# A reordered load phase: layer norms, filler projections and the first V rows in front of a 64-segment recurrence

## The chip, the core and the metric

The kernel runs on one core of a Trainium2 chip. The metric is device time in microseconds (us) of one execution. TensorE is PE below (its weight loads PEld), VectorE is DVE, ScalarE is ACT, GpSimd is POOL, and SyncE is SP, which only issues transfers. Each engine works through its own instructions in the order in which they were recorded. "SPq" or "POOLq" in a profile is the engine's sequencer issuing a transfer.

## What is computed

Two blocks follow one another on x (2048 rows of 512). Block A is attention over 64 segments of 32 rows, with a memory of 8 rows that each segment passes to the next:

```
x1 = layernorm(x)
mem = mem0
for s in 0..63:
    h = concat(mem, x1[32 s : 32 s + 32])            # 40 rows
    q, k, v = h Wq, h Wk, h Wv                       # 32 heads of 128
    p = softmax(mask(q k^T * 128**-0.5))             # 40 x 40 per head
    o = (p v) Wo                                     # 40 x 512
    mem = o[:8];  out_A[32 s : 32 s + 32] = o[8:]
h = x + out_A
```

Block B is a gated feed-forward block with a mixing matrix over the rows: z = gelu(layernorm(h) w_in), the second half of z is normalized, mixed over all 2048 rows by w_sp, increased by b_sp and multiplied with the first half; the result times w_out is added to h. The change does not touch block B.

## The kernel before

**Segments.** A segment's 40 rows are handled as 32 (8 memory rows and the first 24 rows of x) and 8 extended rows (the last 8 of x). The extended rows don't depend on the memory, so their projections are made ahead, for 16 segments at once, a "chunk" of 128 rows (chunks 0 to 3). `hTe` holds a chunk's transposed rows, `QTx` the projected Q and K. A group of `qkx_mm` (L390, matmuls L398) makes 4 heads of Q (i = 0 to 7) or of K (i = 8 to 15) with 16 matmuls; `vx_mm` (L411, matmuls L417) makes 512 columns of V (n = 0 to 7), also with 16. V of the extended rows goes through DRAM to change its layout: `vx_evac` (L421) copies PSUM to SBUF and stores to `vext_d` (L434), and `load_vx` (L439, issue L441) brings one segment's block to `Vx`. Segment s needs 8 consecutive rows of the chunk, that is partitions 8 i to 8 i + 7 of every store, with i = s mod 16.

**Load phase.** SP issues the first x block (L305), Wq in four quarters, the second x block (L308), three further x blocks, the first memory, Wk, Wv and Wo in four quarters each. A quarter is 1 MB and serves 8 heads, that is two groups of `qkx_mm`, or two of `vx_mm`. `ln_inplace` (L349) normalizes one x block: on DVE bn_stats (L352) and bn_aggr (L353), on POOL the reciprocal root (L354, L356), on DVE again the subtraction and multiplication (L358). Statistics alternate between two buffers. `xT` (L361) transposes a block on PE, and ACT copies it out (`xe_copy`, L379, for chunk rows, `ring_copy`, L374, for segment rows).

`start_group` (L710) makes a group into one of the PSUM banks 2, 3, 4, 5 in turn and evacuates it with ACT or DVE in turn; a V group that ACT evacuates is stored through ACT's queue, one that DVE evacuates through POOL's. The loop at L727 runs chunk 0's 16 groups; after group 5 and group 7 it normalizes blocks 1, 4, 5 and 6, and it adds groups 0 to 3 of chunk 1 from group 9 on:

```python
        if i == 5:
            ln_inplace(1)
            ln_inplace(4)
        if i == 7:
            ln_inplace(5)
            ln_inplace(6)
            late_consts()
...
        if i >= 9 and i % 2 == 1:
            start_x(1, i // 2 - 4)
```

**Segment loop.** L821 is written out by hand for all 64 segments. PE does QK (L464, 64 matmuls), the scores (L494 to L509), V (L558), the row sums (L524, L529), the product PV (L575 with the segment's own rows, L581 with `Vx`), the output projection `Wo` (L608), and `mem_out` (L627), whose result ACT writes as the next segment's memory (L630). Segment 0 also makes chunk 0's eight V groups (L842 to L865), issues the first two `load_vx` on POOL (L880), and makes groups 4 to 7 of chunk 1 (L882) ahead of PV. `part_evac` (L619) writes segment s's output to `part[s % 8]`; the same buffers hold chunk 0's V groups on their way to DRAM.

Two lists fill gaps on PE. `gx` (L777, L795 to L799) holds whole groups, one per segment, made ahead of PV into PSUM bank 3 (`XB`) and evacuated by DVE; `gv` (L800) holds V groups of chunks 2 and 3 cut into quarters of 4 matmuls, poured in around `mem_out`. In front of PV in segment 0 stands the first entry of `gx`, V group 0 of chunk 1.

The recording layer (`Emitter`, L34) derives all waits from named reads and writes; an engine waits in front of the instruction that needs them, and everything behind it on that engine waits too. A store through SP stands in SP's order with all other transfers that SP issues.

Of the kernel before, what the change touches and what calls it, by code (L numbers as in the profile page):

```python
# [169 lines left out]
def fast_path(nc, st, keep, A_x, A_mem0, A_Wq, A_Wk, A_Wv, A_Wo, A_seg_len, B_w_in, B_w_sp, B_b_sp, B_w_out, out):  # L170
# [27 lines left out]
    def sb(name, shape, dt):  # L198
        return st.enter_context(nc.sbuf_tensor("f_" + name, shape, dt))
# [42 lines left out]
    stats = sb("stats", [128, 2, 6], F32)  # L242
    mv = sb("mv", [128, RB, 2], F32)
    rstd = sb("rstd", [128, RB], F32)
    st1 = sb("st1", [128, 2, 6], F32)
    mv1 = sb("mv1", [128, 2, 2], F32)
    rs1 = sb("rs1", [128, 2], F32)
    mhalf = sb("mhalf", [128, RB], F32)
    okt = sb("okt", [128, RB], F32)
    okb = sb("okb", [128, 1], BF)  # L250
# [25 lines left out]
    def dve(fn, **k):  # L276
        return em.add("dve", fn, **k)
# [16 lines left out]
    def load_xe(ck, j):  # L294
        t, tok = xbuf(j)
        sp(lambda e: e.dma_start(t, xe[CK * ck:CK * ck + CK, XM:SEG, :]), writes=tok)
# [6 lines left out]
        em.mark_const(("W", mi, hq))  # L303

    load_xe(0, 0)  # L305
    for hq in range(4):
        load_w(0, hq)
    load_xe(1, 1)  # L308
    load_x(0, 4)
    load_x(1, 5)  # L310
    load_xe(2, 6)
# [34 lines left out]
                                                  fill=NEG, base=0, channel_multiplier=-1), reads=["mask"], writes=["mask"])  # L346


    def ln_inplace(j):  # L349
        t, tok = xbuf(j)  # L350
        k = j % 2
        dve(lambda e: e.bn_stats(out=st1[:, k, :], in_=t), reads=tok, writes=[("st1", k)])  # L352
        dve(lambda e: e.bn_aggr(out=mv1[:, k, :], in_=st1[:, k, :]), reads=[("st1", k)], writes=[("mv1", k)])  # L353
        pool(lambda e: e.tensor_scalar(out=rs1[:, k:k + 1], in0=mv1[:, k, 1:2], scalar1=EPS, scalar2=None, op0=ALU.add),  # L354
             reads=[("mv1", k)], writes=[("rs1", k)])
        pool(lambda e: e.tensor_tensor(out=rs1[:, k:k + 1], in0=rs1[:, k:k + 1], in1=mhalf[:, 0:1], op=ALU.pow),  # L356
             reads=[("rs1", k), "mhalf"], writes=[("rs1", k)])
        dve(lambda e: e.tensor_scalar(out=t, in0=t, scalar1=mv1[:, k, 0:1], scalar2=rs1[:, k:k + 1], op0=ALU.subtract, op1=ALU.mult),  # L358
            reads=tok + [("mv1", k), ("rs1", k)], writes=tok)

    def xT(j, bank):  # L361
        t, tok = xbuf(j)
# [58 lines left out]
    def vx_evac(ck, n, bank, eng="act", queue="sp"):  # L421
        if ck == 0:
            t, tok = part[:, n, :], [("part", n, 0), ("part", n, 1)]
        else:
            j = vcnt[0] % 2
            vcnt[0] += 1
            t, tok = Vs[:, j, :], [("Vs", j)]
        if eng == "act":
            act(lambda e: e.activation(out=t, in_=ps[:, bank, :], func=ACT.Copy), reads=[PB(bank)], writes=tok)
        else:  # L430
            dve(lambda e: e.tensor_copy(out=t, in_=ps[:, bank, :]), reads=[PB(bank)], writes=tok)
        b, c = n // 4, n % 4
        dst = vext_d[ck, 4 * c:4 * c + 4, :, b * DH:(b + 1) * DH].rearrange("g t e -> t g e")
        em.add(queue, lambda e: e.dma_start(dst, t.rearrange("p (g e) -> p g e", g=4)), dma=True, reads=tok,  # L434
               writes=[("vext", ck, n)])

    vcnt = [0]

    def load_vx(s, queue="sp"):  # L439
        i = s % CK  # L440
        em.add(queue, lambda e: e.dma_start(Vx[:, s % NVX, :, :], vext_d[s // CK, :, 8 * i:8 * i + 8, :]), dma=True,  # L441
               reads=[("vext", s // CK, n) for n in range(8)], writes=[("Vx", s % NVX)])


    QKB = {(0, 0): 0, (0, 1): 1, (1, 0): 6, (1, 1): 7}
# [253 lines left out]


    act(lambda e: e.preload_act_table_set("natural_log_exp_and_others"))
    ln_inplace(0)
    xT(0, 6)
    xe_copy(0, 6)
    for hq in range(4):
        load_w(1, hq)
    ebank = (2, 3, 4, 5)
# [18 lines left out]

    for i in range(16):  # L727
        start_x(0, i)
        if i == 5:
            ln_inplace(1)  # L730
            ln_inplace(4)
        if i == 7:
            ln_inplace(5)
            ln_inplace(6)
            late_consts()
        if i == 8:
            xT(1, 7)
            xe_copy(1, 7)
        if i == 10:
            xT(4, 6)  # L740
            ring_copy(0, 6)
        if i == 12:
            xT(5, 7)
            ring_copy(1, 7)
        if i == 14:
            xT(6, 6)
            xe_copy(2, 6)
            mem0_transpose(7)
        if i >= 9 and i % 2 == 1:
            start_x(1, i // 2 - 4)  # L750
    for hq in range(4):
        load_w(2, hq)
    wor = A_Wo.rearrange("h e d -> e h d")
# [40 lines left out]

    for n in range(8):  # L795
        vx_group(1, n)
    for ck, i0 in ((1, 8), (2, 0), (3, 0)):
        for i in range(i0, 16):
            qkx_group(ck, i)  # L799
    for ck in (2, 3):  # L800
        for n in range(8):
            vx_atoms(ck, n)


# [16 lines left out]
    for s in range(NSEG):  # L821
        j4 = s % 4
        rb = s // 4
        if j4 == 1 and rb > 0:
            load_h(rb - 1)
        if s == NSEG - 1:
            load_h(rb)
        if s % 2 == 1 and s // 2 < NWT:
            wT_piece(s // 2)
        if j4 == 0 and 2 <= rb + 2 < RB:  # L830
            load_x(rb + 2, 0)
        if s == 4:
            load_xe(3, 1)

        for b in range(2):
            for mi in range(2):
                QK(s, b, mi)
                lastop["qk"[mi]] = em.by_eng["pe"][-1]
                QK_evac(s, b, mi)
        if s == NSEG - 1:  # L840
            load_wT(0, [lastop["q"]])
        if s == 0:  # L842
            for n in range(2):
                start_v(n)
        S_half(s, 0)
        sm_exp(0)
        if s == 0:
            for n in range(2, 4):
                start_v(n)
        V_half(s, 0)  # L850
        V_evac(0, "dve")
        sm_sums(0)
        sm_ln(0)
        S_half(s, 1)
        lastop["s"] = em.by_eng["pe"][-1]
        sm_exp(1)
        if s == NSEG - 1:
            sp(lambda e: e.dma_start(w_in1, winr[:, :, 0:FH]), writes=["w_in1"], after=[lastop["s"], lastop["x"]])
            sp(lambda e: e.dma_start(bsp_b, bass.AP(B_b_sp.tensor, B_b_sp.offset, [[0, 128], [1, S]])), writes=["bsp"], after=[lastop["k"]])
            for r in range(8, RB - 2):  # L860
                xn2T_dma(r, [lastop["s"], lastop["x"]])
        sm_rcp(0)
        if s == 0:
            for n in range(4, 8):
                start_v(n)  # L865
        V_half(s, 1, (0, 1, 2))
        sm_sums(1)
        sm_ln(1)
        sm_rcp(1)
        V_half(s, 1, (3,))  # L870
        lastop["v"] = em.by_eng["pe"][-1]
        V_evac(1, "act")
        sm_norm(0)
        sm_norm(1)
        if s + 1 < NSEG:
            qx_copy(s + 1)
            lastop["x"] = em.by_eng["pool"][-1]
            lastop["x"] = em.by_eng["pool"][-1]
        if s == 0:
            for j in range(2):  # L880
                load_vx(j, "pool")
            for i in range(4, 8):  # L882
                start_x(1, i)
        ev = [gx.pop(0)()] if gx else []
        PV_half(s, 0)
        PV_half(s, 1)
        cT_evac(0, "act")
        cT_evac(2, "dve")
        cT_evac(1, "act")
        cT_evac(3, "dve")  # L890
        for f in ev:
            f()
        if rb > 0:
            WoX_mm(rb - 1, j4)
            if j4 == 3:
                WoX_evac(rb - 1)
        late = []
        Wo((0, 2, 1, 3), OB, 0, OC)
        part_evac(s, OB, 0, OC)
        Wo((0, 2, 1, 3), OB2, OC, D)  # L900
        cTx_copy(s)
        part_evac(s, OB2, OC, D)
        if j4 == 3 and rb > 0:
            F_group(rb - 1, XB)
            WoX_scatter(rb - 1, XB)
            h_done(rb - 1, XB)
        if j4 == 1 and 2 <= rb + 2 < RB:
            ln_inplace(0)
        if s == 5:
            ln_inplace(1)  # L910
        if j4 < 2:
            late += gv.pour(1)
        if j4 == 2 and 2 <= rb + 2 < RB:
            xT(0, XB)
            late.append(lambda: ring_copy(rb + 2, XB))
        if s == 9:
            xT(1, XB)
            late.append(lambda: xe_copy(3, XB))
        if s + 1 < NSEG:
            mem_out(s)  # L920
        late += gv.pour(1)
        for f in late:
            f()
        if s + 2 < NSEG:
            load_vx(s + 2)
        if j4 == 0 and rb >= 2:
            xn2_apply(rb - 2, rb % 2)
            xn2_store(rb - 2, rb % 2)
        if s == 3 * CK:
            free0 = [done47["s"], done47["x"]]  # L930
            sp(lambda e: e.dma_start(w_in2, winr[:, :, FH:F]), writes=["w_in2"], after=free0)
        if 0 <= s - 3 * CK - 1 < 8:
            xn2T_dma(s - 3 * CK - 1, free0)
        if s == 3 * CK - 1:
            done47 = {"s": lastop["s"], "x": px}
        px = lastop.get("x")
# [923 lines left out]
```

## Time and profile before

| | us |
|---|---|
| median of 6 runs | 937.52 (936.33 to 938.69) |
| profiled execution, its own time | 937.35 |
| its span | 935.6 |
| PE busy | 886.2 (95%) |
| DVE, ACT, POOL busy | 447.4, 475.9, 113.0 |
| start of QK of segment 0, 1 and 2 (L464, chain) | 34.50, 62.10, 73.01 |
| weights to landing, one quarter of Wq, Wk, Wv, Wo (median) | 9.6, 13.1, 14.6, 14.7 |
| store of V rows to landing, ACT's queue and POOL's (median) | 8.0 and 6.2 |

The span is the profiled program from its first to its last instruction; the execution's own time is 1.7 us longer. Times inside a profile count from the start of the span. A line of the chain of work has a start, a duration and what ran or what was waited for; a line of the table of waits has the waiting engine and its instruction, what it waited for, the total in us, how often, and the longest. A row of the table by windows has the stretch, its length, busy time and count of instructions for PE, PEld, DVE, ACT and POOL, then the TensorE clock granted (1.00 is full), the share of time in which the 16 DMA engines were busy, and GB/s. A row of DMA queues has the queue (q1 is SP's, q10 ACT's, q0 POOL's), packets, MB and share of the engines' time.

### The profile page before, as it was taken

What the parts mean: (1) busy time and instruction counts of PE and PEld (TensorE: products, weight loads), DVE (VectorE), ACT (ScalarE), POOL (GpSimd) and SP (SyncE); (2) the same over time, 40 slices, a digit from 0 to 9 for tenths busy, and PEclk for the clock granted to TensorE, in tenths of its full rate; (3) what the DMA queues carried; (4) which work ended last, traced back from release to release, by engine and by line L of the source; (5) the groups of instructions that cost most, each with busy time, mean ns of one, the idle gap of its engine ahead of it and who ended that gap; (6) DMA issues with size and microseconds to landing.
All of it is one profiled execution on the core that took longest, in us unless ns stands there. A gap on an engine that the chain in (4) does not pass through costs nothing.

```text
span 935.6 us, 45477 instructions
## 1 busy us (share of the span) xinstructions
PE 886.2 (95%) x20966; PEld 488.1 (52%) x20973; DVE 447.4 (48%) x1033; ACT 475.9 (51%) x1154; POOL 113.0 (12%) x280
## 2 busy tenths in 40 slices
PE   5979999999999999999999999998999899999997
PEld 5745555555555555555555555454444444444443
DVE  3435455555554545555555555444434454453443
ACT  2435666666556666666666656565656565400000
POOL 1511111111111111111101111111101021200000
PEclk9999999999999999999999999999999999999999
DMA  9942312131303122121303120413111293021201
GB/s 327 374 137 49 72 48 60 46 74 26 71 19 74 40 57 43 49 60 38 71 25 63 46 66 21 116 32 77 39 52 53 71 274 103 1 93 47 87 12 36
DMA packets 101524, 71.29 MB, mean 76 GB/s; under 512 B 60200, under 2 KB 86704, under 8 KB 101328
## 3 DMA queue, kind: packets, MB, share of 16 engines
q1 hardware_dynamic: 98960, 67.14, 26.0%
q8 instruction: 166, 2.72, 1.3%
q10 hardware_dynamic: 2112, 0.52, 0.3%
q0 software_dynamic: 256, 0.66, 0.2%
q14 instruction: 30, 0.25, 0.1%
HBM read 39.46 MB, written 18.61 MB: 62 GB/s over the span
## 4 chain that ended last, share of the span: by engine, by line
PE 90%; ACT 4%; DMA 2%; issue 2%; DVE 1%; SPq 1%; POOL 0%; POOLq 0%
PE f_ps L464 25%; PE f_ps L608 13%; PE f_ps L558 11%; PE f_ps L1003 10%; PE f_ps L398 6%; PE f_ps L652 4%; PE f_ps L965 3%; PE f_ps L575 3%; PE f_ps L996 3%; PE f_ps L1073 2%; PE f_ps L627 2%; PE f_ps L417 2%; PE f_ps L503 2%; ACT f_hT L630 1%; PE f_ps L524 1%
## 5 line engine op out<-in xcount | busy, mean ns | idle before, releaser
L464 PE MATMUL f_ps<-f_arena,f_hT 128*32 128x512 bf16 x4096 | 232.7, 380 | 9.5 <-ACT f_hT L630 6.5
L471 ACT ACTIVATE f_Tst<-f_ps 128x512 bf16<-128x512 f32 x256 | 152.8, 597 | 109.2 <-PE f_ps L464 108.6
L464 PEld LDWEIGHTS f_ps<-f_arena,f_hT 128*32 128x32 bf16 x4096 | 103.6, 97 | 121.7 <-ACT f_hT L630 24.1
L477 DVE STREAM_TRANSPOSE f_QT<-f_Tst 128x256 uint32<-128x256 uint32 x128 | 57.0, 445 | 176.3 <-ACT f_Tst L471 176.3
L558 PE MATMUL f_ps<-f_arena,f_hT 128*32 128x512 bf16 x2048 | 140.1, 378 | 0.0
L608 PE MATMUL f_ps<-f_arena,f_cT 128*32 128x384 bf16 (+1 forms) x4096 | 125.2, 275 | 3.1 <-ACT f_cT L594 2.2
L608 PEld LDWEIGHTS f_ps<-f_arena,f_cT 128*32 128x32 bf16 x4096 | 84.7, 97 | 61.8 <-ACT f_cT L594 31.6
L1003 PE MATMUL f_ps<-f_arena 128*128 128x512 bf16 x448 | 101.3, 379 | 2.5 <-DVE f_arena L1009 1.6
L620 ACT ACTIVATE f_part<-f_ps 128x384 bf16<-128x384 f32 (+1 forms) x128 | 46.4, 384 | 75.8 <-PE f_ps L608 75.8
L480 DVE STREAM_TRANSPOSE f_KT<-f_Tst 128x256 uint32<-128x256 uint32 x128 | 57.0, 445 | 52.7 <-ACT f_Tst L471 52.7
L596 DVE TENSOR_SCALAR f_cT<-f_ps 128x320 bf16<-128x320 f32 x128 | 56.9, 487 | 42.1 <-PE f_ps L581 42.1
L398 PE MATMUL f_ps<-f_hTe,f_arena 128*128 128x128 bf16 x1024 | 69.6, 227 | 5.2 <-DMA f_arena<-in_A_Wk_dram 2.2
L487 POOL COPY f_QT<-f_arena 128x256 bf16<-128x256 bf16 x64 | 30.7, 480 | 357.4 <-PE f_ps L509 357.3
L1003 PEld LDWEIGHTS f_ps<-f_arena 128*128 128x128 bf16 x448 | 43.5, 98 | 56.0 <-DVE f_arena L1009 2.6
L398 PEld LDWEIGHTS f_ps<-f_hTe,f_arena 128*128 128x128 bf16 x1024 | 61.6, 102 | 15.6 <-issue 12.4
L594 ACT ACTIVATE f_cT<-f_ps 128x320 bf16<-128x320 f32 x128 | 49.0, 435 | 39.2 <-PE f_ps L581 39.2
L544 DVE SCALAR_TENSOR_TENSOR f_E_sb<-f_R_sb,f_E_sb 128x160 bf16<-128x160 f32 x128 | 41.7, 326 | 46.1 <-ACT f_R_sb L540 46.1
L536 ACT ACTIVATE f_R_sb<-f_ps 128x160 f32<-128x160 f32 x128 | 38.8, 303 | 37.5 <-PE f_ps L529 37.5
L558 PEld LDWEIGHTS f_ps<-f_arena,f_hT 128*32 128x32 bf16 x2048 | 44.8, 95 | 21.5
L616 POOL COPY f_cTx<-f_cT 128x256 bf16<-128x256 bf16 x64 | 26.1, 408 | 196.2 <-DVE f_cT L596 196.2
L1009 DVE TENSOR_TENSOR f_arena<-f_ps,f_arena 128x512 f32<-128x512 f32 x28 | 19.3, 690 | 57.8 <-PE f_ps L1003 57.8
L575 PE MATMUL f_ps<-f_E_sb,f_V_sb 32*128 32x40 bf16 x2048 | 36.2, 177 | 10.5 <-DVE f_E_sb L549 9.0
(103 smaller groups left out, 1092.3 us busy)
## 6 DMA issues: line engine op xcount, KB each, us to landing
wT_d<-f_wst SPq DMA_DIRECT2D x32, 256.0 KB, 2.3
f_arena<-wT_d SPq DMA_DIRECT2D x32, 256.0 KB, 4.6
f_arena<-in_A_Wq_dram SPq DMA_DIRECT2D x4, 1024.0 KB, 9.6
f_arena<-in_A_Wk_dram SPq DMA_DIRECT2D x4, 1024.0 KB, 13.1
f_arena<-in_A_Wv_dram SPq DMA_DIRECT2D x4, 1024.0 KB, 14.6
f_arena<-in_A_Wo_dram SPq DMA_DIRECT2D x4, 1024.0 KB, 14.7
f_Vx<-vext_d SPq DMA_DIRECT2D x62, 64.0 KB, 2.6
vext_d<-f_Vs SPq DMA_DIRECT2D x24, 128.0 KB, 2.0
```

The costliest lines, as they stand in the source:

```text
L398: pe(lambda e, h=h, dc=dc, hh=hh: e.matmul(ps[:, bank, hh * 128:(hh + 1) * 128], lhsT=ws[:, dc, h * DH:(h + 1) * DH], rhs=hTe[:, ck % 3, d ...
L464: pe(lambda e, dc=dc, c=c, rhs=rhs: e.matmul(ps[32 * c:32 * c + 32, bank, :], lhsT=hT[:, sl, dc, :], rhs=rhs, start=(dc == 0), stop=(dc == ...
L471: act(lambda e: e.activation(out=Tst[:, tb, :].rearrange("p (hp i r) -> p hp i r", i=32, r=2), in_=ps[:, bank, :].rearrange("p (hp r i) -> ...
L477: dve(lambda e: e.transpose(out=dst, in_=src), reads=[("T", tb)], writes=[("QT", b)])
L480: dve(lambda e: e.transpose(out=dst, in_=src), reads=[("T", tb)], writes=[("KT", b)])
L558: pe(lambda e, dc=dc, c=c, c0=c0: e.matmul(ps[32 * c:32 * c + 32, bank, :], lhsT=hT[:, sl, dc, :], rhs=w_v[:, dc, c0:c0 + 512], start=(dc ...
L575: pe(lambda e, q=q, c=c, g=g, c0=c0: e.matmul(ps[:, PVB[c], c0:c0 + 40], lhsT=V_sb[q, b, g * 128:(g + 1) * 128], rhs=E_sb[q, b, g * 40:(g ...
L594: act(lambda e: e.activation(out=dst, in_=src, func=ACT.Copy, scale=UNSC), reads=[PB(PVB[c])], writes=[("cT", c)])
L596: dve(lambda e: e.tensor_scalar(out=dst, in0=src, scalar1=UNSC, scalar2=None, op0=ALU.mult), reads=[PB(PVB[c])], writes=[("cT", c)])
L608: pe(lambda e, h=h, g=g, i=i, b=b, c=c: e.matmul(ps[32 * g:32 * g + 32, bank, 0:d1 - d0], lhsT=cTh[:, i, 8:40], rhs=w_o[:, h, d0:d1], star ...
L620: act(lambda e: e.activation(out=part[:, s % 8, d0:d1], in_=ps[:, bank, 0:d1 - d0], func=ACT.Copy), reads=[PB(bank)], writes=[("part", s % ...
L1003: pe(lambda e: e.matmul(ps[:, bank, 0:TB], lhsT=z2[:, sc, fb * 128:(fb + 1) * 128], rhs=wTb[tb % 2][:, :, sc, :], start=(sc == 0), stop=(s ...
```

## The change

Five things move; no matmul and no transferred byte of the results is added or left out.

- The second x block is issued ahead of Wq instead of behind it.
- `ln_inplace` is cut into `ln_stats` (both DVE statistics and POOL's part) and `ln_apply`, with three statistics buffers instead of two. Blocks 0 and 1 are normalized and transposed together ahead of the loop; the statistics of blocks 4, 5 and 6 stand together after group 8, and the three applies after groups 9, 10 and 11.
- Chunk 1's groups 0 to 7 are made in the loop, one behind each odd group of chunk 0, in place of groups 0 to 3 behind groups 9, 11, 13 and 15. Segment 0 then makes groups 8 and 9 of chunk 1 in place of 4 to 7.
- Each of the eight stores of chunk 0's V is cut in two: partitions 0 to 15 (the rows of segments 0 and 1) go on the queue that took the whole before, ACT's or POOL's; partitions 16 to 127 go on SP's, where they stand behind Wo and one x block. `load_vx` of segments 0 and 1 waits for the first parts only; from segment 2 on it waits for both.
- In `gx`, groups 8 and 9 of chunk 1 are replaced by V groups 0 and 1 of chunk 2, which leave `gv`: `gx` keeps 48 entries, and `gv` has 56 quarters instead of 64.

```diff
     load_xe(0, 0)
+    load_xe(1, 1)
     for hq in range(4):
         load_w(0, hq)
-    load_xe(1, 1)
...
-    def ln_inplace(j):
+    def ln_stats(j):
         t, tok = xbuf(j)
-        k = j % 2
+        k = j % 3
...
+    def ln_apply(j):
+        t, tok = xbuf(j)
+        k = j % 3
         dve(lambda e: e.tensor_scalar(out=t, in0=t, scalar1=mv1[:, k, 0:1], scalar2=rs1[:, k:k + 1], op0=ALU.subtract, op1=ALU.mult),
             reads=tok + [("mv1", k), ("rs1", k)], writes=tok)
+
+    def ln_inplace(j):
+        ln_stats(j)
+        ln_apply(j)
...
-        em.add(queue, lambda e: e.dma_start(dst, t.rearrange("p (g e) -> p g e", g=4)), dma=True, reads=tok,
-               writes=[("vext", ck, n)])
+        for k, (i0, i1) in enumerate(((0, 2), (2, CK)) if ck == 0 else ((0, CK),)):
+            r = slice(8 * i0, 8 * i1)
+            em.add("sp" if k else queue, lambda e, r=r: e.dma_start(dst[r], t[r].rearrange("p (g e) -> p g e", g=4)), dma=True,
+                   reads=tok, writes=[("vext", ck, n, k)])
...
-               reads=[("vext", s // CK, n) for n in range(8)], writes=[("Vx", s % NVX)])
+               reads=[("vext", s // CK, n, k) for n in range(8) for k in range(2 if 2 <= s < CK else 1)], writes=[("Vx", s % NVX)])
...
-    ln_inplace(0)
-    xT(0, 6)
-    xe_copy(0, 6)
+    for j in range(2):
+        ln_stats(j)
+    for j in range(2):
+        ln_apply(j)
+        xT(j, 6 + j)
+        xe_copy(j, 6 + j)
...
         start_x(0, i)
-        if i == 5:
-            ln_inplace(1)
-            ln_inplace(4)
-        if i == 7:
-            ln_inplace(5)
-            ln_inplace(6)
+        if i % 2 == 1:
+            start_x(1, i // 2)
+        if i == 8:
+            for j in range(4, 7):
+                ln_stats(j)
             late_consts()
-        if i == 8:
-            xT(1, 7)
-            xe_copy(1, 7)
+        if i in (9, 10, 11):
+            ln_apply(i - 5)
...
-        if i >= 9 and i % 2 == 1:
-            start_x(1, i // 2 - 4)
...
-    for ck, i0 in ((1, 8), (2, 0), (3, 0)):
+    for ck, i0 in ((1, 10), (2, 0), (3, 0)):
+        if ck == 2:
+            vx_group(2, 0)
+            vx_group(2, 1)
...
-    for ck in (2, 3):
-        for n in range(8):
+    for ck, n0 in ((2, 2), (3, 0)):
+        for n in range(n0, 8):
             vx_atoms(ck, n)
...
-            for i in range(4, 8):
+            for i in range(8, 10):
                 start_x(1, i)
```

The transposes of blocks 4, 5 and 6 and their copies keep their places, after groups 10, 12 and 14.

## The prediction

> **What bounds the kernel now.** I read the page first: PE is busy 95% of the span, so time is lost only where PE waits. The table of PE's waits from 0 to 60 us puts nearly all large ones into the load phase:
>
> ```profile
> PE f_ps L581 <- DMA f_Vx<-vext_d: 3.7, 1, 3.7
> PE f_ps L398 <- DMA f_arena<-in_A_Wk_dram: 2.2, 1, 2.2
> PE f_ps L398 <- DMA f_arena<-in_A_Wq_dram: 2.0, 2, 1.6
> ```
>
> (waiter, waited for: total us, times, longest). A wait removed early pays only if no later wait is set by something else, so I read the chain that ended last, in order of time:
>
> ```profile
> 9.61 11.16 DMA f_arena<-in_A_Wk_dram
> ...
> 20.91 1.87 PE f_ps L398 x16
> ...
> 34.50 3.57 PE f_ps L464 x64
> ...
> 46.20 8.08 DMA vext_d<-f_part
> 54.28 0.03 POOLq L158
> 54.31 0.51 issue
> 54.82 2.17 DMA f_Vx<-vext_d
> 56.99 0.05 issue
> 57.03 0.21 PE f_ps L581 x4
> ...
> 57.93 3.31 PE f_ps L608 x64
> ...
> 70.21 1.93 PE f_ps L608 x64
> ```
>
> (start, us, what). Two gates: Wk's first quarter at 20.8, and a longer one at 57.03, when the first V block of the extended rows (Vx) arrives. Behind it the 64 segments run at a fixed beat: the chain's first QK matmuls (L464) stand at 62.10, 73.01, 83.92. **The filler costs nothing there:** by the timeline four segments from 445.9 take 43.9 us (PE busy 43.5 in the window of them), and four from 664.7, without filler groups, take 43.6 (PE busy 39.4). So whatever moves in or out of the later segments is worth about 0, and the change is worth what it does to 57.03, plus or minus the clock after it.
>
> **Load phase, up to QK of segment 0.** The second x block (128 KB) is now issued ahead of Wq. SP's rows start 0.74 us apart, and 128 KB at the 385 GB/s of that stretch are 0.34 us; so the first projection moves from 8.09 by 0.34 to 0.74, and I take 8.5. The layer norm of block 0 is not delayed: its subtract waits for POOL until 5.41 now, and the second block's statistics (0.69 + 0.18 us) fit into that wait. If the second block lands after 4.5, its cost still hides in the wait for Wq.
>
> The four groups of chunk 1 (16 matmuls each) fill the waits for Wq and Wk. A group takes 0.89 us at full clock (48 matmuls in 2.68) and 1.70 at first: ACT evacuates groups 0 and 2 at 9.99 and 13.40, and the matmul count per us jumps from 13 to 22 at 14.0. So 5.5 us give 3.2 groups, and the other 8.8 of the twelve take 7.8: PE ends them at 21.8, after Wk's landing (20.8), without a stop. That is 0.9 later than PE begins Wk's groups now, but it then runs at full clock, where the row at 20.91 shows 1.87 us for 16:
>
> ```profile
> 20.50:21.00 0.50, 0.09 (x2) 0.12 (x3) 0.00 (x0) 0.00 (x0) 0.42 (x2) 0.73 1.04 385
> 21.00:21.50 0.50, 0.50 (x7) 0.50 (x7) 0.28 (x1) 0.00 (x0) 0.18 (x1) 0.50 1.03 377
> 24.50:25.00 0.50, 0.50 (x13) 0.50 (x10) 0.50 (x1) 0.00 (x0) 0.00 (x0) 1.00 1.05 389
> ```
>
> (windows: PE busy and count first; the granted clock is the third number from the end.)
>
> **A new wait.** All three statistics of blocks 4, 5, 6 now stand together on DVE, between the evacuation of the last filler group and that of group 9, and apply 4 comes behind that. In DVE's timeline a statistics pair takes 0.93 us (24.37 to the next free slot), an evacuation 0.69, an apply 0.41. From 21.8: evacuation to 22.6, three pairs to 25.3, evacuation to 26.0, apply to 26.5. PE wants that block's transpose after groups 8, 9, (1,4), 10, that is 3.6 us, at 25.4. It waits 1.1 us, and everything is queued behind it, as PE runs in order. Bounds: 0 if PE is held up elsewhere by as much, 2 if DVE also waits for POOL's rstd. Behind it come eight groups (7.15) and the transposes (3 x 0.22 + 0.18): QK starts at 34.5, where it starts now. The freed transpose of block 1, the filled waits and the kept clock are given back by the late filler and this wait.
>
> **Between QK and the gate.** V's groups keep their order and times. Two chunk-1 groups stand there instead of four: -1.8 us. The next V group writes bank 3, which the second of them has just used, so it waits for that evacuation on DVE: +0.8 (0.69 and its start), where bank 3 was free before. PE finishes its first PV part at 53.36 now; it will at 52.4. The 1.0 us wait for ACT at 48.4 stays, since the same bank follows. All that PE gains here is hidden unless Vx comes sooner.
>
> **When Vx comes.** The load on POOL now waits for eight stores of 16 partitions instead of 128; the other 112 go to SP's queue, behind Wo. What the store of 8.08 us consists of: the window 39.6 to 43.8 has no packet of ACT's queue though its first store was issued at 39.61, and packets run from 43.9; with idle DMA the store issued at 59.02 has its first packet at 59.9. So 4.3 against 0.9 us pass before the first byte, 3.4 of it for the Wo traffic. Then:
>
> ```profile
> q1 hardware_dynamic: 528, 0.53, 73.3%
> q10 hardware_dynamic: 496, 0.12, 26.7%
> ```
>
> (43.9 to 46: SP's queue and ACT's, packets, MB, share.) The two alternate, some 240 packets of ACT's per us. A whole store (512) is 2 us, and the last stands behind the one before it; a small one (64) is 0.3. The small ones lose the queueing and keep the 3.4: ACT's last, issued at 46.2, lands after 4.3 + 0.3 + 0.9 for the tail, at 51.7. POOL's last is issued at 47.46 and takes 6.2 now (the median of the DMA table); bounds are 1.9, the landing of an undisturbed store, and 6.2. I take 5.3, close to the loaded row, since only its own data shrink: 52.8. Then POOL's wake and issue 0.54 and the load, 2.17 alone, up to 5.6 with the 3.4 of first-byte wait. The moved stores are the traffic it can meet: between 43.9 and 54.2 ACT's and POOL's queues have 22.8% and 12.9% of the engines' time, 3.7 us, seven eighths of which (3.2) leave the front. Wo so ends near 50.9 instead of 54.1 and the moved part near 54.1, while the load's first byte is due 1.2 us after 53.3. Hence close to the lower end, 2.3: **Vx at 55.6 instead of 57.03, -1.4 us.** Part 0, which segment 0 overwrites at about 59, is stored long before.
>
> The clock: after the gap now the window 58.3 to 61.6 shows 0.50, and Wo takes 3.31 instead of 1.93. The remaining gap, 52.4 to 55.6, is 3.2 us, longer than the 2.2 us gap at 18.7 that also ended at 0.50; so that loss stays. SP waits for the moved stores before its load for segment 2, due only near 80.
>
> **Two rules of the Trainium skill.** "DMA: Bandwidth & Descriptors", Rules for kernel authors, speaks against splitting one transfer over disjoint partitions: both parts share the same engines. By it Vx would come at 57.0 and the time stay 937.3; but the row above puts the cost into queueing of whole stores, which the split shortens. "TensorE: Matmul & The Clock Gate", Part 1, has the clock fall after an idle window of about 3.4 us. By that the remaining gap could leave the clock whole and save 1.4 more (an estimate: 934.5); the row at 20.91, half clock after 2.2 us, speaks against it.
>
> **Sum.** The profiled execution took 937.35 us (span 935.6, 1.7 around it), 0.2 below the median 937.52. 937.35 - 1.4 = **935.9**.
>
> **Rivals.**
> - *The stores become quick and the gate opens* (chance 0.25). If the first-byte wait shrinks with the traffic, POOL's last lands 1.9 after 47.46, and Vx comes at 52.1; then PE's 52.4 decides: -4.6, and with the gap gone the clock's 1.4 too: 931.4. Halfway, Vx at 54: 934.3. For it: Wo's queue is shorter. Against: the medians of POOL's and ACT's stores under that traffic are 6.2 and 8.0.
> - *It doesn't do what it says* (0.18). The late filler and DVE's statistics push V's stage back by 1.4 more, so stores are issued later by what they save: 937.3. For it: DVE's row sum above; against: the V stage needs no weights that come late.
> - *Slower: the Vx load meets the moved stores* (0.12). They run in SP's queue when the load starts. Were its first byte 3.4 us late, as under Wo, Vx would come at 53.3 + 5.6 = 58.9: +1.9, and a gap of 6.5 us leaves the clock low up to 0.6 longer: 939.8. It decides once the load takes more than 3.7. Against it: 512 such packets pass in under 1 us at 59.9.
>
> **How the numbers follow.** My forecast has 0.45. 0.2% (1.9 us) is about what a measurement of this kernel can tell from no change; the forecast lies 1.6 below the median, just inside. Its own bounds, 934.4 to 937.4, fall a third on the faster side. Faster: 0.25 + 0.15 = 0.40; same: 0.30 + 0.18 + 0.02 = 0.50; slower 0.10. The range leaves out the gate fully open and the full collision: 933.3 to 938.4.
>
> **What would show it.** Right: no PE wait for Wk, clock 1.00 at 21; a wait of about 1 us of a transpose for the apply; QK near 34.5; L581 still waiting 3 us for Vx, released near 55.6; beat of 10.9 unchanged. Wrong: PV without a wait, small stores landing 2 us after issue, or QK a us or more off 34.5.

## The result and the profile after

The changed kernel takes 934.71 us (median of 20 runs, 933.01 to 937.06), the kernel before in the same comparison 937.45 (42 runs). The ratio is 0.997, interval [0.9964, 0.9977]: 2.7 us faster, where 1.6 below the median was forecast, and inside the range given (933.3 to 938.4). The profiled execution took 934.4 us with a span of 932.7, against 937.35 and 935.6.

PE's waits from 0 to 60 us in the kernel after (waiter, waited for: total us, times, longest):

```profile
PE f_ps L592 <- DMA f_Vx<-vext_d: 2.9, 1, 2.9
PE f_ps L406 <- ACT f_V_sb L576: 1.1, 1, 1.1
PE f_ps L425 <- DVE f_arena L417: 0.8, 1, 0.8
...
PE f_ps L372 <- DVE f_part L362: 0.4, 1, 0.4
```

The line numbers have moved: L406 is a projection group (L398 before), L372 a transpose, L425 a V group, L592 the product with `Vx`. The waits for Wk are gone, and of those for Wq 0.2 us are left. Two waits are new: a transpose for DVE's apply (L362), 0.4 us, and a V group for the evacuation of PSUM bank 3 (L417), 0.8. The wait for `Vx` is still the largest but for the start.

The chain that ended last, in order of time, in the same profile (start, us, what):

```profile
7.85 13.16 PE f_ps L406 x192
21.04 0.69 DVE f_arena L417
21.73 0.61 DVE f_st L352
22.37 0.18 DVE f_mv L353
22.55 0.59 DVE f_st L352
23.16 0.18 DVE f_mv L353
23.34 0.59 DVE f_st L352
23.95 0.18 DVE f_mv L353
24.14 0.57 DVE f_arena L417
24.71 0.34 DVE f_part L362
...
25.09 0.40 PE f_ps L372 x4
...
33.37 3.57 PE f_ps L475 x64
...
46.30 4.87 DMA vext_d<-f_part
...
51.45 2.63 DMA f_Vx<-vext_d
...
54.13 0.24 PE f_ps L592 x3
...
55.07 3.60 PE f_ps L619 x64
...
70.89 3.64 PE f_ps L475 x64
```

The first piece is the twelve groups (192 matmuls) in one run, without a stop for weights. Then the chain goes through DVE: an evacuation, three pairs of statistics back to back, an evacuation, the apply. QK of segment 0 (L475) starts at 33.37 instead of 34.50. One chain of 16-partition stores, a POOL wake and a load leads to the gate at 54.13 instead of 57.03. Of these 2.9 us, 2.1 are left at QK of segment 2 (70.89 against 73.01): the clock took back 0.8.

Windows of the kernel after (window, its length, busy us and count of PE, PEld, DVE, ACT, POOL, granted clock, DMA share, GB/s), first at Wk's landing, then behind the gate:

```profile
20.00:22.00 2.00, 2.00 (x38) 1.92 (x36) 0.96 (x2) 0.60 (x1) 0.00 (x0) 1.00 1.04 384
...
56.00:57.00 1.00, 1.00 (x20) 0.51 (x16) 0.14 (x1) 0.00 (x0) 0.01 (x1) 0.50 0.00 0
```

At 21 us the clock is now full. Behind the gate it is at half from 53.60 to 60.43, 6.83 us, where before it was 3.41 us; so segment 0's output projection and the start of segment 1 run slowly.

DMA issues of the first 62 us in the kernel after (out<-in, queue, count, KB each, median us to landing; before, ACT's stores took 8.0, POOL's 6.2 and the load 2.2):

```profile
f_Vx<-vext_d POOLq DMA_DIRECT2D x2, 64.0 KB, 2.6
...
vext_d<-f_part ACTq DMA_DIRECT2D x4, 16.0 KB, 5.5
vext_d<-f_part POOLq DMA_DIRECT2D x4, 16.0 KB, 5.4
```

An eighth of the bytes still takes over 5 us to land. Most of that is time before the first packet: between 45.2 and 46.9 ACT's queue has no packet at all, though its store issued at 45.08 is under way; that store lands 5.4 us after its issue.

### The profile page after: what moved, and what is told of

Its sections match the earlier page's. It is cut to its first block, busy times and chain, and to the rows that moved or that the text cites. A ratio compares the mean times of both kernels' runs of the same rounds, so it can differ in the third digit from the quotient of the medians.

```text
span 932.7 us, 45493 instructions
## 1 busy us (share of the span) xinstructions
PE 886.1 (95%) x20966; PEld 487.0 (52%) x20973; DVE 447.9 (48%) x1034; ACT 475.8 (51%) x1153; POOL 112.9 (12%) x280
## 4 chain that ended last, share of the span: by engine, by line
PE 91%; ACT 4%; DVE 2%; issue 2%; DMA 1%; SPq 0%; POOL 0%
PE f_ps L475 25%; PE f_ps L619 13%; PE f_ps L569 11%; PE f_ps L1016 10%; PE f_ps L406 6%; PE f_ps L663 4%; PE f_ps L586 3%; PE f_ps L978 3%; PE f_ps L1009 3%; PE f_ps L1086 2%; PE f_ps L638 2%; PE f_ps L425 2%; PE f_ps L514 2%; ACT f_hT L641 1%; PE f_ps L535 1%
## 5 line engine op out<-in xcount | busy, mean ns | idle before, releaser
L475 PE MATMUL f_ps<-f_arena,f_hT 128*32 128x512 bf16 x4096 | 233.2, 380 | 10.6 <-ACT f_hT L641 8.0
L475 PEld LDWEIGHTS f_ps<-f_arena,f_hT 128*32 128x32 bf16 x4096 | 103.7, 97 | 122.1 <-ACT f_hT L641 24.2
L406 PE MATMUL f_ps<-f_hTe,f_arena 128*128 128x128 bf16 x1024 | 67.0, 223 | 1.3 <-ACT f_V_sb L576 1.1
L406 PEld LDWEIGHTS f_ps<-f_hTe,f_arena 128*128 128x128 bf16 x1024 | 59.7, 100 | 11.0 <-issue 9.5
L555 DVE SCALAR_TENSOR_TENSOR f_E_sb<-f_R_sb,f_E_sb 128x160 bf16<-128x160 f32 x128 | 41.7, 325 | 46.2 <-ACT f_R_sb L551 46.2
```

Of the source, the lines that this page charges most:

```text
L406: pe(lambda e, h=h, dc=dc, hh=hh: e.matmul(ps[:, bank, hh * 128:(hh + 1) * 128], lhsT=ws[:, dc, h * DH:(h + 1) * DH], rhs=hTe[:, ck % 3, d ...
L475: pe(lambda e, dc=dc, c=c, rhs=rhs: e.matmul(ps[32 * c:32 * c + 32, bank, :], lhsT=hT[:, sl, dc, :], rhs=rhs, start=(dc == 0), stop=(dc == ...
```

## The experiments

Theory: the change gains through the landing of the first V rows, which two things move together, the earlier issue (load phase) and the smaller stores (split); the clock after the gap is an extra loss. Rivals: that one of the two alone makes the gain; that the small stores wait for Wo's stream and so land when it lets them; that the moved stores delay the load. Ratios are against the kernel before, run on the same chip: median 936.88 (29 runs) for the first four, 937.0 (11) for the next four, 937.32 (9) for the last two.

**The split alone** (e1_split_only). The kernel before, with only the divided stores and the load's reads:

```diff
-        em.add(queue, lambda e: e.dma_start(dst, ...), writes=[("vext", ck, n)])
+        for k, (i0, i1) in enumerate(((0, 2), (2, CK)) if ck == 0 else ((0, CK),)):
+            r = slice(8 * i0, 8 * i1)
+            em.add("sp" if k else queue, lambda e, r=r: e.dma_start(dst[r], ...), writes=[("vext", ck, n, k)])
```

> The kernel before with the store split alone; load phase, layer norms and filler lists as before. Theory (the arrival of the first Vx block is the gate, and the load phase and the split each shorten the way to it): QK of segment 0 stays at 34.5; POOL's last small store, issued at 47.5, lands after 4.9 as it does in the changed kernel, so Vx comes at about 55.2 instead of 57.0: -1.8 us, 935.6 to 935.7. The gap of PE shrinks from 3.7 to 1.9 us, so in some executions the clock may stay full and up to 1.3 more is saved. Rival 1 (the load phase alone makes the gain, the split is hidden behind the same traffic): 937.4. Rival 2 (the split alone makes it): 934.7.

Measured: 936.0 us (11 runs), ratio 0.999 [0.998, 1.0]. Its chain:

```profile
48.50 4.57 DMA vext_d<-f_part
...
53.36 3.26 DMA f_Vx<-vext_d
...
56.66 0.24 PE f_ps L584 x3
```

The last small store lands after 4.57 us, but it is issued only at 48.50: the load phase of this execution ran at half clock from 19.1 to 25.9 (twice as long as in the profile before), and QK came at 35.20. From QK to the gate it took 21.5 us, against 22.5 before and 20.8 after. By the medians the split alone is worth 0.9 us, half of the 1.8 expected; its interval takes in both nothing and the 1.8.

**The load phase alone** (e2_no_split). The kernel after, with whole stores:

```diff
-        for k, (i0, i1) in enumerate(((0, 2), (2, CK)) if ck == 0 else ((0, CK),)):
...
+        em.add(queue, lambda e: e.dma_start(dst, ...), writes=[("vext", ck, n)])
```

> The changed kernel with chunk 0's V stored whole, as before. Theory: QK of segment 0 at 33.4, all stores 1.1 us earlier than before, ACT's last whole store lands after 8.1 again, so Vx comes at 55.9 instead of 57.0: -1.1 us, 936.3. PE reaches the gate at 51.3 and waits 4.6. Rival 1 (load phase alone): 934.7. Rival 2 (split alone): 937.4.

Measured: 936.67 us (11 runs), ratio 0.9998 [0.9989, 1.0006]. Its chain, and below it PE's wait:

```profile
45.16 8.64 DMA vext_d<-f_part
...
54.33 2.16 DMA f_Vx<-vext_d
...
56.54 0.24 PE f_ps L589 x4
```

```profile
PE f_ps L589 <- DMA f_Vx<-vext_d: 5.2, 1, 5.2
```

QK starts at 33.45, 0.1 later than in the kernel after (33.37), but the whole store takes 8.64 us and lands at 53.80, 0.5 earlier than before (54.28). The early start turns into a longer wait (5.2 instead of 3.7), and the longer gap costs two slow clock stretches instead of one. So neither part alone is shown to carry the gain: by the medians they are worth 0.9 and 0.2 us alone and 2.7 together, and only the two together have an interval that lies wholly and clearly below 1. The traces say why the load phase gains little by itself: with whole stores the last one is issued 1.0 earlier than before and lands only 0.5 earlier, and the clock takes half of that. That the two gains are more than additive is likely by the medians (1.1 against 2.7) but not sure: the interval of the split alone reaches down to 0.998, that is 1.9 us.

**V earlier** (e3_v_earlier). Four of the late filler groups go back behind V in segment 0:

```diff
-        if i % 2 == 1:
+        if i % 2 == 1 and i < 8:
             start_x(1, i // 2)
...
-            for i in range(8, 10):
+            for i in range(4, 10):
```

> The changed kernel, but groups 4 to 7 of chunk 1 leave the load phase again and stand behind V in segment 0, ahead of groups 8 and 9. Theory: QK of segment 0 starts near 31.0 (it can't be earlier, as Wk's last quarter lands at 28.8), V's last store is issued about 2 us earlier, and PE's gap fills with groups. What Vx gains depends on the traffic: the stores and now also the Vx load run under Wo; with 2.6 us for the load Vx comes at about 52 (932.6 or less, since the gap closes and the clock stays full), with 3.4 us more for its first byte at about 55 (935). Rival (everything small lands when Wo's stream ends near 51, whenever it was issued): Vx at 54, 934.7 or up to 1.5 less if the clock stays full.

Measured: 933.71 us (12 runs), ratio 0.9969 [0.9957, 0.9981], the changed kernel's own within its interval. The chain:

```profile
44.92 5.58 DMA vext_d<-f_part
...
50.78 3.12 DMA f_Vx<-vext_d
```

QK came at 31.62, 1.8 earlier, the last store is issued 1.4 earlier, and the gate opens 0.2 earlier, at 53.94. The store takes 0.7 longer and the load 0.5. The rival is right here in what counts: an earlier issue is taken back by the transfers.

**The gap filled** (e4_gap_filled). Groups 8 to 12 of chunk 1, instead of 8 and 9, ahead of the gate; the later segments' list gets five V groups of chunk 2 in their place:

```diff
-    for ck, i0 in ((1, 10), (2, 0), (3, 0)):
+    for ck, i0 in ((1, 13), (2, 0), (3, 0)):
...
-            for i in range(8, 10):
+            for i in range(8, 13):
```

> The changed kernel with three more groups of chunk 1 (10 to 12) in segment 0 ahead of PV, replaced in the filler list by three V groups of chunk 2. Theory: the gate stays at 54.1, PE reaches it near 53.2 instead of 51.3 and idles 1 us, so the clock stays at 1.00; segment 0's rest takes 4.0 instead of 5.6 us and segment 1 10.9 instead of 11.3: -1.3 to -2.0 against the changed kernel, 933. Rival (the clock after the gap doesn't matter, the recurrence hides it): 934.7. If the fill ends after the gate: up to 0.5 slower than theory.

Measured: 932.38 us (5 runs), ratio 0.9956 [0.9943, 0.9969]. PE's wait for `Vx`:

```profile
PE f_ps L592 <- DMA f_Vx<-vext_d: 1.3, 1, 1.3
```

The gate stands at 53.92 as in the kernel after, so the extra groups cost nothing in front of it, and QK of segment 2 comes at 69.68 instead of 70.89. The clock still falls, for 3.41 us instead of 6.83. The second profile of the kernel after (below) has the same 69.72, so part of these 1.2 us is the spread of the clock; against that profile the gain, 0.9 us, appears in the later segments (QK of segment 60 at 704.79 instead of 705.65).

**Wo held back** (e5_wo_held). Wo's four quarters are issued only when the first two `Vx` blocks have landed:

```diff
+            vxl = [load_vx(j, "pool") for j in range(2)]
+            for hq in range(4):
+                sp(lambda e, hq=hq: e.dma_start(w_o[:, 8 * hq:8 * hq + 8, :], ...), writes=[("Wo", hq)], after=vxl)
```

> The changed kernel with Wo's four loads issued only when the first two Vx blocks have landed; its whole time is then set by a later Wo, and only the way to the gate is read. Theory (Wo's stream is what the small stores wait for): POOL's last small store lands about 2 us after its issue instead of 4.9, Vx's load takes 2.2, so Vx is there by about 51, before PE asks for it, and the wait of 2.9 at the gate is gone; Wo then lands from 54 on, the last quarter near 63, so 8 to 9 us more in all. Rival (the latency belongs to the stores, 16 partitions and 256-byte rows): 4.9 and a gate at 54 as now.

Measured: 944.97 us in one run, slower because PE then waits for Wo (13.3 us in all). Its DMA issues of the first 62 us, and PE's waits to 75 us:

```profile
vext_d<-f_part ACTq DMA_DIRECT2D x4, 16.0 KB, 1.8
vext_d<-f_part POOLq DMA_DIRECT2D x4, 16.0 KB, 1.9
```

```profile
PE f_ps L619 <- DMA f_arena<-in_A_Wo_dram: 13.3, 3, 5.8
...
PE f_ps L592 <- DMA f_Vx<-vext_d: 0.2, 1, 0.2
```

The same small stores land in 1.8 and 1.9 us instead of 5.5 and 5.4, and the gate opens at 51.66, 0.2 us after PE gets there. This shows that Wo's stream on SP's queue is what the stores on the two other queues wait for. The first `Vx` load is not quicker for it: issued at 48.57, with Wo not yet issued and the last moved store landed, it takes 3.0 us.

**The moved stores held back** (e6_moved_held). The 112-partition stores are issued behind the two loads:

```diff
+            if k:
+                moved.append(store)
+            else:
+                store()
...
+            vxl = [load_vx(j, "pool") for j in range(2)]
+            for f in moved:
+                f(vxl)
```

> The changed kernel with the eight moved stores (partitions 16 to 127) issued by SP only behind the first two Vx loads. Theory (the Vx load of 2.6 to 3.3 us meets the moved stores, alone it takes 2.2): -0.4 us at the gate, 934.2, against the changed kernel's 934.7 beside 937.4. Rival (the load meets nothing): 934.7. If the first moved store came too late for segment 0's part buffer (57.9) there would be a new ACT wait and up to 1 us more.

Measured: 933.84 us (6 runs), ratio 0.9959 [0.9946, 0.9972]. The chain:

```profile
46.30 4.81 DMA vext_d<-f_part
...
51.40 2.07 DMA f_Vx<-vext_d
```

The store is as slow as with the moved stores in the queue (4.87), the load is 0.56 faster, and the gate stands at 53.52. In a second profile of the kernel after the load took 2.17 with the moved stores in place, so not more than some 0.5 us, and not in every execution, is theirs. The time, 0.9959, can't be told from that of the kernel after.

**Statistics earlier** (e7_stats_early). The three statistics go behind groups 6, 7 and 8, one each:

```diff
+        if i in (6, 7, 8):
+            ln_stats(i - 2)
         if i == 8:
-            for j in range(4, 7):
-                ln_stats(j)
             late_consts()
```

> The changed kernel with the statistics of blocks 4, 5 and 6 one each behind groups 6, 7 and 8 instead of together behind group 8. Theory: PE's wait of 0.4 us for the apply of block 4 goes and QK starts 0.4 earlier, at 32.9; but small stores issued earlier land no earlier while Wo streams, so the gate moves by 0 to 0.4 only: 934.3 to 934.7. Rival (every us of the load phase comes through): -0.4, 934.3.

Measured: 933.87 us (5 runs), ratio 0.9965 [0.9952, 0.9978]. PE no longer waits for the apply, and QK starts at 32.67. Its wait for `Vx`:

```profile
PE f_ps L592 <- DMA f_Vx<-vext_d: 3.5, 1, 3.5
```

The gate stands at 54.03: 0.7 won ahead of QK, 0.1 at the gate, and 0.6 more of waiting (3.5 instead of 2.9). Where an earlier issue goes is the same in six profiles: in those of the kernel after, e3, e4, e7 and e8 the first `Vx` load is issued at 50.78 to 51.70 and lands at 53.81 to 54.09, and the earliest issued takes the longest (3.12 and 3.18 us at 50.78 and 50.80, 2.17 at 51.70).

**Filled up to the gate** (e8_fill_to_gate). As in the filled gap, but with groups 8 to 14 and seven V groups of chunk 2 moved:

```diff
-            for i in range(8, 10):
+            for i in range(8, 15):
```

> The changed kernel with groups 8 to 14 of chunk 1 in segment 0 ahead of PV (seven instead of two; seven V groups of chunk 2 take their places in the list of whole groups). Theory: PE now arrives at about 54.2, as Vx does, so no wait is left and the clock stays 1.00 through segment 0's rest, which takes 3.9 instead of 5.4 us: 2.0 less than the changed kernel, 0.7 less than with groups 8 to 12: 931.7 to 932.3 beside a before of 937. Rival (the clock falls anyway, or the added group only delays PV): 932.5 to 933.5.

Measured: 932.64 us (6 runs), ratio 0.9954 [0.9942, 0.9966]. The chain:

```profile
46.82 6.43 PE f_ps L406 x112
53.24 0.98 PE f_ps L425 x16
...
55.17 1.93 PE f_ps L619 x64
```

No DMA stands in the chain at the gate any more: PE itself arrives at 54.27. The clock stays at 1.00, so segment 0's output projection takes 1.93 us instead of 3.60, and QK of segment 1 comes at 57.97, 1.6 earlier than in the kernel after (59.55) and 0.8 earlier than in its second profile (58.80). This is one execution, and the fastest of the six (930.67 us, mean granted clock 1.000); the others have a mean clock of 0.997 to 0.999, so in them it fell somewhere.

**Three at once** (e9_combined). Filled to the gate, the moved stores held, the statistics early; the edits are those above.

> The changed kernel with all three edits that gained: groups 8 to 14 of chunk 1 in segment 0, the statistics of blocks 4 to 6 spread behind groups 6 to 8, and the moved stores held behind the first Vx loads. Theory: the stores land near 50.5, Vx near 53.0 instead of 54.1, PE arrives near 53.5 without a stop and with the clock at 1.00, so QK of segment 1 starts near 57.2 instead of 59.6: about 2.4 to 2.8 us less than the changed kernel on the same chip, some 0.7 less than the filled gap alone. Rival (with the gap closed only PE's own work counts, so the held stores add nothing): 0.7 from the statistics alone, and a new wait for the late stores in segment 0's output copy costs up to 1 us.

Measured: 932.45 us (5 runs), ratio 0.9955 [0.9941, 0.9968], the same as with the fill alone. The chain:

```profile
53.68 0.98 PE f_ps L425 x16
...
55.60 1.93 PE f_ps L625 x64
```

Once PE sets the gate, a sooner `Vx` is worth nothing. The early statistics should then show at QK, but it came at 33.35, since full speed began only at 13.71 us in this execution (12.64 in the kernel after's).

**The kernel after once more** (after_again), to be compared with the last one.

> The changed kernel itself, beside the combined one on the same chip. Expected -2.7 us against before (0.997), gate near 54.1 in its profile; the start of the clock's windows differs from one execution to the next, so its cold stretch may lie elsewhere.

Measured: 933.7 us (5 runs), ratio 0.9961 [0.9947, 0.9975]. Its chain:

```profile
46.44 4.97 DMA vext_d<-f_part
...
51.70 2.17 DMA f_Vx<-vext_d
...
69.72 3.64 PE f_ps L475 x64
```

Gate at 53.92, wait for `Vx` 2.5 us, half clock behind the gate for 3.41 us only, QK of segment 2 at 69.72. The best versions, those that fill the gap, are at 0.9954 to 0.9956, 4.4 to 4.9 us below the kernel before, each beside its own runs of it; the kernel after is 2.7 and 3.6 below, so filling the gap is worth 0.7 to 2.1 us more. Their intervals overlap with the first one of the kernel after at the end and with the second nearly wholly, so that they beat it is likely, not sure.

## Why the prediction was right, and where it was off

- **First projection.** Predicted 8.5, measured 7.85 (8.09 before). Over the profiles of both orders it lies between 7.15 and 8.16, so the 0.4 us for the second x block ahead of Wq do not show.
- **Twelve groups.** Predicted end 21.8, behind Wk's landing and at full clock; measured 21.04, no wait and 1.00. The mechanism held. Of the 0.8, 0.65 is the earlier start.
- **The wait for DVE.** This is the term that was mis-sized. Predicted 1.1 us; measured 0.4. The pair of statistics was put at 0.93 from a pair that stood by itself in the profile before; back to back the pairs follow one another at 0.79 (22.55 to 23.34). DVE's whole run from the end of the groups to the transpose takes 4.05 us (21.04 to 25.09) instead of 4.7: 0.3 of the difference are the pairs, the rest the evacuations and the apply, which also follow without gaps. The wait for POOL's rstd, the upper bound's reason, does not show in the chain.
- **QK.** Predicted "where it starts now", 34.5; measured 33.37. The transpose of block 4 comes at 25.09 instead of the predicted 26.5: 0.8 by the earlier end of the groups and 0.7 by the shorter wait; from there to QK it is 8.3 us instead of 8.0. Statistics spread over three groups (e7) are worth another 0.7 ahead of QK.
- **PE between QK and the gate.** Predicted 52.4 and 0.8 us for bank 3; measured 51.2 (earlier by as much as QK) and 0.8. The 1.0 us wait for ACT stayed, as said (1.1).
- **Stores and load.** Predicted: POOL's last takes 5.3 and lands 5.3 after 47.46, the load 2.3, `Vx` at 55.6. Measured: issued at 46.30, 4.87, load 2.63, 54.13. ACT's last store was put at 5.5 us (46.2 to 51.7) and took 5.4. That the small stores keep a wait under Wo is shown by the run with Wo held, 1.8 instead of 5.5 us, and that they lose the queueing by the run with whole stores, 8.64 instead of 5.4 for ACT's last. Of the 1.5 us by which the gate is earlier than predicted, 1.2 are the earlier issue, 0.4 the faster store and 0.3 POOL's wake and issue (0.28 instead of 0.54), against 0.3 of a slower load.
- **The clock.** "That loss stays": it stayed, and was twice as long in this profile. In the second profile of the kernel after it was as long as before, and QK of segment 2 is 3.3 us earlier instead of 2.1. This is the spread of single executions; the median gain of 2.7 lies between. The reason given for the loss was the length of the gap; the stretches below show the share of PE's work in fixed stretches instead.
- **The beat.** The segments keep their 10.9 us, but that moved filler is worth 0 was not quite so: 0.5 us are given back by segment 60 (1.63 earlier there instead of 2.12). By the starts of QK, segments 13, 24, 42 and 47 take 0.2 to 0.4 us longer in both profiles of the kernel after (segment 42: 11.12 and 11.13 against 10.95), while 11 and 18 are shorter in both (11.18 in 18 before, 11.00 and 10.95 after). What makes these segments longer was not tried.
- **The sum.** Two errors of the same sign, in the load phase and in the stores (1.5 us at the gate), stand against 0.8 of clock and 0.5 of filler. So at QK of segment 60 this profile is 1.6 earlier than before, near the forecast's 1.4 by errors that cancel; the second one, with the short clock loss, is 2.7 earlier (705.65 against 708.34), as the median of the first comparison is. That the forecast of the time was near is so in part luck: at the gate the gain was 2.9 us, twice the 1.4 predicted. The spans of before and after still differ by 2.95, since the profile before has one 1.0 us stall of PE in the last segments (L608, released by nothing that the profile shows) that the one after lacks; why is not known. The second profile of the kernel after has a span of 932.7 too, as it lost 3.41 us to half clock a second time, from 828.63, in block B.

The rivals. *The gate opens fully*: not so with Wo's stream (4.87, not 1.9), but so without it (e5: PE waits 0.2 us). *It does not do what it says*: the V stage was not pushed back, as POOL's last store was issued at 46.30, 1.2 earlier than before. *The Vx load meets the moved stores*: at most by 0.6 us (2.63 against 2.07 in this pair, 2.17 in the second profile), not by the 3.4 that would have made the kernel slower.

Against the rule in the Trainium skill, "DMA: Bandwidth & Descriptors", Rules for kernel authors (no split of one transfer over disjoint partitions, since the parts share the engines): an eighth of the bytes did not land in an eighth of the time, but the rows needed first stood behind fewer of them. With the split the store that lands last takes 4.87 us (POOL's), without it 8.64 (ACT's), the last landing moves from 53.80 to 51.17, and the ratio goes from 0.9998 [0.9989, 1.0006] to 0.997 [0.9964, 0.9977].

Not settled: why the load takes 2.07 in one execution and 3.26 in another (with the moved stores held it took 2.07 in e6 and 2.06 in e9, but 3.0 in e5 with neither them nor Wo in the way), and why the same store takes 5.58 when it is issued at 44.92 and 4.87 at 46.30.

## What to carry to other kernels

When a wait is set by a transfer that stands behind a bulk stream, an earlier start and a smaller transfer may have to come together: here early stores that were whole mostly waited longer, and small stores were late when their issue was. Price a chain of such steps at the gate, not at the step where the time is won, and ask at each step what is late next. A gap in PE's work that can't be closed from the side of the data may take work that has to be done anyway: here the medians show another 0.7 to 2.1 us for it.

## What the runs showed of the hardware

**Small transfers under a stream.** Stores of 16 KB on ACT's and POOL's queues need 5.5 and 5.4 us while SP's queue carries Wo, and 1.8 and 1.9 while it does not. Splitting a store takes away its length and its place behind other long stores, but not this wait.

**The clock changes at fixed stretches of 3.41 us.** In the twelve profiles of this study the granted clock changes only at multiples of 3.41 us from its first rise, and what PE did in one stretch goes with the clock of the next. What it takes differs with the clock in the stretch itself:

| kernel, stretch (us) | clock in it | PE busy in it | clock in the next |
|---|---|---|---|
| after, 50.19 to 53.60 | 1.00 | 1.09 | 0.50 |
| before, 17.32 to 20.73 | 1.00 | 1.41 | 0.50 |
| e4, 52.17 to 55.58 | 1.00 | 1.52 | 0.50 |
| e3, 51.61 to 55.02 | 1.00 | 1.78 | 0.50 |
| before, 51.45 to 54.87 | 1.00 | 1.92 | 1.00 |
| after, 46.78 to 50.19 | 1.00 | 2.13 | 1.00 |
| e8, 52.62 to 56.03 | 1.00 | 2.87 | 1.00 |
| e1, 19.10 to 22.51 | 0.50 | 1.88 | 0.50 |
| e7, 53.19 to 56.60 | 0.50 | 2.06 | 0.50 |
| after, 53.60 to 57.01 | 0.50 | 2.37 | 0.50 |
| after_again, 53.80 to 57.22 | 0.50 | 2.79 | 1.00 |
| e6, 53.71 to 57.12 | 0.50 | 2.88 | 1.00 |

Four of these rows as the windows have them (same columns as above), the first from the profile before, the second from the second profile of the kernel after, the others from its first:

```profile
51.45:54.87 3.42, 1.92 (x46) 1.06 (x43) 0.69 (x1) 0.48 (x1) 0.05 (x1) 1.00 0.54 180
53.80:57.22 3.42, 2.79 (x56) 1.53 (x60) 1.49 (x3) 0.77 (x2) 0.40 (x1) 0.50 0.50 101
50.19:53.60 3.41, 1.09 (x32) 0.38 (x24) 0.00 (x0) 0.00 (x0) 1.07 (x2) 1.00 1.01 248
53.60:57.01 3.41, 2.37 (x52) 1.26 (x56) 1.49 (x3) 0.77 (x2) 0.40 (x1) 0.50 0.41 97
```

Over the twelve profiles the full clock was kept after every stretch with 1.9 us of PE work or more and lost after those with 1.78 or less, but for two in block B that kept it (before, 829.69 to 833.10, 1.58; e8, 824.03 to 827.44, 1.63); so busy time is not the whole of it. From half clock it took more to regain it: 2.37 us did not do, 2.79 did. No stretch without work is needed to lose it. The Trainium skill, "TensorE: Matmul & The Clock Gate", Part 1, has the clock fall after an idle window of about 3.4 us, and here it fell after stretches in which PE was busy for half of the time (e3: 1.78 of 3.41).

Whether one or two slow stretches follow the same gap depends on where it lies in the raster. In the second profile of the kernel after the raster stands 0.2 us later and the gate 0.2 earlier, so the stretch behind the gate has 2.79 us of work instead of 2.37, and the clock stays low for 3.41 us instead of 6.83. Four of the twelve profiles (e1, e2, e6, after_again) lost 3.41 us also between 828 and 836 us, in block B, which the change does not touch. The times follow: of the executions of the kernel after on record, the three with a mean granted clock of 0.993 or 0.994 took 936.6 to 937.1 us, the three with 0.998 took 933.0 to 933.8.

**Half pace while the clock column shows 1.00.** At the start PE's matmuls are slow though the column shows 1.00. Windows of the kernel after:

```profile
8.00:12.00 4.00, 4.00 (x40) 4.00 (x39) 0.54 (x1) 0.88 (x2) 0.00 (x0) 1.00 1.05 390
...
14.00:16.00 2.00, 2.00 (x40) 2.00 (x38) 0.91 (x2) 0.60 (x1) 0.00 (x0) 1.00 1.07 383
```

40 matmuls take 4.00 us, and later 2.00. The column has no record ahead of the first rise (10.65 to 13.91 us, by execution), and these 3.3 us of spread at half pace are 1.6 us of work (an estimate). A difference of a microsecond between two single profiles should be checked against that first.
